# Attention of a fused attention and MLP kernel in 64-row and 64x64 TensorE tiles, with k and v loaded in two halves by two queues

## The chip, the cores and the metric

One core of a Trainium2 chip runs the whole kernel. The metric is the device time of one execution in microseconds (us). A run is called slow when it lies over 1.5% above the fastest run of the same kernel, and fast otherwise; fast runs are compared with fast runs taken in the same rounds of measurement.

## The reference

Eight batches of eight heads attend 576 queries to 72 pooled keys (means of eight neighbours), then an MLP with a tanh shrink follows. All tokens are independent in the MLP.

```python
B, H, S, D = q.shape                       # 8, 8, 576, 64
k_p = k.reshape(B, H, 72, 8, D).mean(axis=3)
v_p = v.reshape(B, H, 72, 8, D).mean(axis=3)
scores = np.matmul(q, k_p.transpose(0, 1, 3, 2)) / np.sqrt(D)
attn = softmax(scores)                     # cut: max, exp, sum
x = np.matmul(attn, v_p)                   # to (4608 tokens, 512)
h = x @ w_in                               # 512 -> 2048
out = (h - np.tanh(h)) @ w_out             # 2048 -> 512
```

## The kernel before

The MLP goes in nine groups of 512 tokens; one group is called a round here (round 0 is the start). A round has 64 wide matmuls for `h` and 64 for `o`. Between the `o` matmuls of round g the attention of batch g+1 is interleaved, for batches 2 to 7. GpSimd pools k and v; q, k and the attention result x are transposed by DMA.

```python
    def load_k(b):                                    # v: the same, with four small pieces
        return [
            load_main(k_pairs, k_raw[b % 2], b, 0, NM),   # 128 of the 144 rows of each pair of heads
            load_dense(k_pairs, k_raw[b % 2], b),         # the 16 rows left of each pair
        ]
    ...
    def score_mms(b, t, dst, c0, c1, pairs=range(NM)):
        for m in pairs if t == NM else (t,):
            ...                                       # KB: block-diagonal, two heads a tile
            nc.tensor.matmul(dst[p : p + w], lhsT=KB[b % 2][:, o : o + w],
                             rhs=qTs[b][:, m, c0:c1], start=True, stop=True)
    ...
    def av(b, blk, alloc, by_dma):                    # 2 x 3 matmuls of 130 columns a block
        x_sb = new_x()
        for half in range(2):
            av_half(b, blk, half, x_sb, alloc)        # matmuls, reciprocal, division
        if by_dma:
            ...
            nc.sync.dma_start_transpose(out=xT[:, :, pos : pos + 128 - p0], in_=...)
    ...
                if i == (3 if g == 1 else 8):         # in the h part of round g
                    k_dma_transpose(nb)
                    k_place(nb, nc.gpsimd.tensor_copy)
                    if nb + 1 < B:
                        load_k(nb + 1)
                        load_v(nb + 1)
                        load_q(nb + 1)
    ...
                    if 1 <= u <= NT:                  # in the o part, slot u of 16
                        scores(nb, u - 1)
                    if u in (7, 8, 9, 10, 12):
                        av(nb, (7, 8, 9, 10, 12).index(u), ps_b1, True)
```

The softmax here doesn't subtract the row's maximum and nothing guards it: scores larger than these inputs give would overflow.

## Time and profile before

| | before |
|---|---|
| median time | 300.64 us (300.51 to 300.65; a fourth run, beside the change, 301.79) |
| TensorE busy | 97% |
| next engine, VectorE | 53% |
| a round with attention | 30.81 us |
| of it the MLP | 27.63 us |

"Busy" of TensorE overlaps matmul with matmul, so distances between starts are the honest measure. The first lines are the DMA issues of the kernel before (name, issuing queue, count, size, median time to landing). Then come two stretches of four microseconds, with these columns: the stretch, its length, busy time and count of TensorE, its weight loads, VectorE, ScalarE and GpSimd, the granted clock, the DMA share and GB/s.

```profile
k_raw<-in_k_dram SPq DMA_DIRECT2D x7, 1024.0 KB, 5.9
q_raw<-in_q_dram SPq DMA_DIRECT2D x7, 1024.0 KB, 10.2
...
72.00:76.00 4.00, 4.00 (x28) 1.80 (x26) 0.00 (x0) 3.17 (x9) 0.00 (x0) 1.00 1.06 329
76.00:80.00 4.00, 4.00 (x34) 2.40 (x32) 2.31 (x9) 0.70 (x2) 1.15 (x1) 1.00 1.06 293
```

The loads of the next batch keep all DMA engines busy (share about 1) at some 300 GB/s while TensorE works on. They are hidden, but they are not idle time.

### The profile page before, as it was taken

To read this page: it belongs to the slowest core of one execution; us is meant where nothing else is said; L and a number is where in the kernel's file an instruction comes from. 1 tells how busy PE (TensorE), PEld (TensorE's weight loads), DVE (VectorE), ACT (ScalarE), POOL (GpSimd) and SP (SyncE) were. 2 spreads that over 40 slices of the span, in tenths; PEclk is the share of its full clock that TensorE was granted. 3 is DMA by queue.
4 is the path that set the end of the run, shared out by engine and by line. 5 is a ranking of instruction groups with operands and counts; after the bars stand their busy time and mean duration, and the time that the engine had idled before them with its cause. 6 is when DMAs were issued, how large, how long until landed. Compare 5 with 4: busy or idle time off the path is not lost.

```text
span 299.1 us, 4694 instructions
## 1 busy us (share of the span) xinstructions
PE 291.5 (97%) x1671; PEld 142.5 (48%) x1671; DVE 159.1 (53%) x343; ACT 149.4 (50%) x283; POOL 115.5 (39%) x110
## 2 busy tenths in 40 slices
PE   7989999999999999999999999999999999999994
PEld 3454455544544454445444554455445544444443
DVE  5658665673547444753476247716680758108600
ACT  4647583666146633654265516650665166126511
POOL 8500904871496109922971089307940000000000
PEclk9999999999999999999999999999999999999999
DMA  7999999849854998699648974897431430111032
GB/s 251 226 211 278 311 227 310 263 87 328 234 113 99 271 297 134 117 302 245 107 88 235 300 167 94 242 294 159 97 66 35 95 92 0 37 70 36 0 72 70
DMA packets 66183, 49.79 MB, mean 166 GB/s; under 512 B 39920, under 2 KB 52976, under 8 KB 66160
## 3 DMA queue, kind: packets, MB, share of 16 engines
q1 hardware_dynamic: 58832, 42.94, 56.0%
q0 software_dynamic: 4752, 4.72, 9.4%
q10 hardware_dynamic: 2576, 1.84, 2.3%
q8 instruction: 13, 0.21, 0.3%
q14 instruction: 10, 0.08, 0.1%
HBM read 36.70 MB, written 9.44 MB: 154 GB/s over the span
## 4 chain that ended last, share of the span: by engine, by line
PE 85%; DMA 9%; POOL 4%; issue 0%; SPq 0%; ACT 0%; DVE 0%; POOLq 0%
PE o_ps L456 40%; PE hT_ps L428 37%; DMA w1b<-in_moe_w_in_dram 4%; PE x_ps L346 4%; DMA k_raw<-in_k_dram 4%; PE s_ps L298 3%; POOL k_raw L198 1%; DMA out_dram<-o_sb 1%; POOL k_raw L203 1%; POOL kd L206 1%; POOL w2b L510 0%; PE xT_ps L390 0%; POOL v_raw L576 0%; PE qT_ps L171 0%; POOL w1b L503 0%
## 5 line engine op out<-in xcount | busy, mean ns | idle before, releaser
L456 PE MATMUL o_ps<-w2b,gT 128*128 128x512 bf16 x560 | 134.4, 380 | 0.0
L441 DVE TENSOR_TENSOR gT<-hT_ps,t_sb 128x512 bf16<-128x512 f32 x144 | 98.9, 691 | 57.7 <-ACT t_sb L439 57.6
L428 PE MATMUL hT_ps<-xT,w1b 128*128 128x512 bf16 x576 | 126.9, 379 | 0.3 <-ACT xT L397 0.3
L439 ACT ACTIVATE t_sb<-hT_ps 128x512 f32<-128x512 f32 x144 | 85.6, 597 | 38.3 <-PE hT_ps L428 37.5
L428 PEld LDWEIGHTS <-w1b 128*128 128x128 bf16 x576 | 55.9, 98 | 66.5 <-issue 0.4
L456 PEld LDWEIGHTS <-gT 128*128 128x128 bf16 x560 | 52.5, 98 | 52.0 <-issue 1.4
L465 ACT COPY o_sb<-o_ps 128x512 f32<-128x512 f32 x33 | 19.3, 585 | 75.2 <-PE o_ps L456 75.2
L359 DVE RECIPROCAL rden<-x_ps 128x4 f32<-128x4 f32 x80 | 14.2, 177 | 52.5 <-PE x_ps L346 52.0
L360 DVE TENSOR_TENSOR x_sb<-x_ps,rden 128x256 bf16<-128x256 f32 x80 | 34.0, 425 | 3.5 <-DMA xT<-x_sb 0.6
L148 POOL CAST q_bf<-q_raw 128x2048 bf16<-128x2048 f32 x6 | 11.3, 1888 | 59.9 <-issue 34.8
L198 POOL TENSOR_TENSOR k_raw<-k_raw 128x1280 f32<-128x1280 f32 x7 | 20.2, 2886 | 27.4 <-DMA k_raw<-in_k_dram 16.6
L317 ACT ACTIVATE E<-s_ps 128x288 bf16<-128x288 f32 x60 | 21.4, 410 | 13.2 <-PE s_ps L298 13.0
L346 PE MATMUL x_ps<-VB,E 128*128 128x130 bf16 x240 | 20.8, 221 | 0.4 <-ACT xT L397 0.3
L346 PEld LDWEIGHTS <-E 128*128 128x128 bf16 x240 | 16.9, 98 | 8.8 <-DVE VB L230 0.6
L216 POOL TENSOR_TENSOR v_raw<-v_raw 128x1280 f32<-128x1280 f32 x6 | 17.4, 2898 | 0.0
L298 PE MATMUL s_ps<-qT,KB 128*128 128x288 bf16 (+5 forms) x128 | 17.0, 290 | 0.2
L298 PEld LDWEIGHTS <-KB 128*128 128x128 bf16 (+1 forms) x128 | 7.0, 96 | 10.2 <-issue 3.5
L527 PE MATMUL warm_ps<-xT 128*128 128x512 bf16 x29 | 10.2, 465 | 1.3 <-DVE xT L539 1.3
L206 POOL TENSOR_TENSOR kd<-k_raw 128x640 bf16<-128x640 f32 x7 | 10.8, 1540 | 0.5
L203 POOL TENSOR_TENSOR k_raw<-k_raw 128x640 f32<-128x640 f32 x7 | 10.8, 1541 | 0.5
L397 ACT CAST xT<-xT_ps 128x256 bf16<-128x256 f32 (+1 forms) x14 | 5.8, 436 | 8.5 <-PE xT_ps L390 5.1
L219 POOL TENSOR_TENSOR v_raw<-v_raw 128x640 f32<-128x640 f32 x6 | 9.3, 1544 | 0.5
(73 smaller groups left out, 100.7 us busy)
## 6 DMA issues: line engine op xcount, KB each, us to landing
k_raw<-in_k_dram SPq DMA_DIRECT2D x7, 1024.0 KB, 5.9
q_raw<-in_q_dram SPq DMA_DIRECT2D x7, 1024.0 KB, 10.2
v_raw<-in_v_dram SPq DMA_DIRECT2D x7, 1024.0 KB, 9.3
out_dram<-o_sb SPq DMA_DIRECT2D x38, 128.0 KB, 2.4
out_dram<-o_sb SPq DMA_DIRECT2D x16, 256.0 KB, 3.7
w1b<-in_moe_w_in_dram POOLq DMA_DIRECT2D x4, 512.0 KB, 14.2
w2b<-in_moe_w_out_dram POOLq DMA_DIRECT2D x4, 512.0 KB, 16.9
k_raw<-in_k_dram SPq DMA_DIRECT2D x7, 128.0 KB, 5.8
```

What stands on the lines that cost most here:

```text
L198: first = eng.tensor_tensor(out=r[:, :, 0:4, :], in0=r[:, :, 0:4, :], in1=r[:, :, 4:8, :], op=ALU.add)
L216: eng.tensor_tensor(out=r[:, :, 0:4, :], in0=r[:, :, 0:4, :], in1=r[:, :, 4:8, :], op=ALU.add)
L298: nc.tensor.matmul(dst[p : p + w], lhsT=KB[b % 2][:, o : o + w], rhs=qTs[b][:, m, c0:c1], start=True, stop=True,)
L317: nc.scalar.activation(out=E[:, t, half * hs : (half + 1) * hs], in_=ps[:, :], func=ACT.Exp, scale=SCALE)
L346: nc.tensor.matmul(ps[:, 2 * n : 2 * n + 2, :].rearrange("p h d -> p (h d)") if n < 2 else ps.rearrange("p (a s) d -> p a s d", s=2)[:, :, ...
L359: nc.vector.reciprocal(out=rden[:, :, :], in_=ps[:, :, D:D1])
L360: nc.vector.tensor_tensor(out=x_sb[:, half, :, :], in0=ps[:, :, 0:D], in1=rden[:, :, :].to_broadcast([128, 4, D]), op=ALU.mult,)
L428: nc.tensor.matmul(h_tiles[i][:, :], lhsT=w1b[:, fb, i * 128 : (i + 1) * 128], rhs=xT[:, fb, tok0 : tok0 + TG], start=(fb == 0), stop=(fb ...
L439: nc.scalar.activation(out=t_sb[:, :], in_=h_ps[:, :], func=ACT.Tanh)
L441: nc.vector.tensor_sub(out=gT[:, :], in0=h_ps[:, :], in1=t_sb[:, :])
L456: nc.tensor.matmul(o_ps[:, :], lhsT=gts[i][:, tb * 128 : (tb + 1) * 128], rhs=w2b[:, i, :], start=(i == 0), stop=(i == NHID - 1),)
L465: (nc.vector.tensor_copy if g == 0 and tb % 2 else nc.scalar.copy)(out=o_sb[:, :], in_=o_ps[:, :])
```

## The change

The intent is to use the array better. A score tile of the kernel before has only two useful 64x64 blocks, so four heads go into four 64x64 tiles at once; AV contracts 64 rows, so two heads go into the two row halves at once. As each change of tile shape costs a drain, the work is gathered into four bursts a batch. For this each head must sit on one half of the partitions with 64 of its 72 rows. The source of such a tile has a hole of eight rows in the middle: as one pattern it would have four dimensions instead of three. The change issues k and v as two transfers of 64 partitions each, one by each of two queues. In batch 0, division runs over two PSUM banks at a time.

```diff
+    k_main = k_rows.rearrange("b (t i g) n -> b i g t n", i=2, g=G)[:, :, 0:GM]
+    v_main_rows = v_rows.rearrange("b (i t g) n -> b i g t n", i=2, g=G)[:, :, 0:GM]
...
+    def load_halves(src, left, dst, b):
+        for i, eng in enumerate((nc.sync, nc.gpsimd)):
+            yield eng.dma_start(out=dst[64 * i : 64 * i + 64, 0:NM, :], in_=src[b, i])
+        yield nc.sync.dma_start(out=dst[::2, NM, :], in_=left[b])
...
-        nc.sync.dma_start(
-            out=t[:, :, 0:R, :], in_=q[b, :, 0:QA, :].rearrange("h (p j) d -> p h j d", j=R)
-        )
+        n = H // 2 if b > 1 else H
+        for h in range(0, H, n):
+            nc.sync.dma_start(...)                     # q in two transfers of four heads
...
+    def score_main(b, j, dst, c0, c1):
+        for s, i in ((0, 0), (1, 1), (0, 1), (1, 0)):
+            m = j + 2 * i
+            nc.tensor.matmul(
+                dst[s][64 * i : 64 * i + 64],
+                lhsT=kTs[b][64 * s : 64 * s + 64, m, 64 * s : 64 * s + 64],
+                rhs=qTs[b][64 * s : 64 * s + 64, m, c0:c1],
...
+    def av_tiles(b, blk, pss):                         # 4 pairs of 65 columns, 1 pair of 260
+        ...
+                lhsT=E[64 * i : 64 * i + 64, t, c0 : c0 + 128],
...
-                    if 1 <= u <= NT:
-                        scores(nb, u - 1)
-                    if u in (7, 8, 9, 10, 12):
-                        av(nb, (7, 8, 9, 10, 12).index(u), ps_b1, True)
+                    if u in (2, 5):
+                        scores_pairs(nb, u // 3)
+                    if u in (7, 10):
+                        av_stream(nb, (0, 1, 2) if u == 7 else (3, 4))
```

Cut: the masks of the left-over rows, the pooling of v without duplicates, the fixed PSUM banks, and batch 0.

More of the change, by code (lines that the diff above doesn't have):

```diff
@@ L33 @@
 NM = 4
+GM = 64
+GL = 2 * (G - GM)
 SCALE = 1.0 / (POOL * float(D) ** 0.5)
@@ L57, with bank, __init__, tile @@
     opool = ctx.enter_context(tc.tile_pool(name="opool", bufs=4))
-    ps_h = ctx.enter_context(tc.tile_pool(name="ps_h", bufs=3, space=PSUM))
-    ps_o = ctx.enter_context(tc.tile_pool(name="ps_o", bufs=2, space=PSUM))
-    ps_a = ctx.enter_context(tc.tile_pool(name="ps_a", bufs=3, space=PSUM))
+    psum = ctx.enter_context(tc.tile_pool(name="psum", bufs=1, space=PSUM))
+    PS = psum.tile([128, 8, 512], FP32, name="PS")
+    def bank(i, shape):
+        n = 1
+        for d in shape[1:]:
+            n *= d
+        v = PS[:, i, 0:n]
+        if len(shape) == 3:
+            return v.rearrange("p (a b) -> p a b", a=shape[1])
+        if len(shape) == 4:
+            return v.rearrange("p (a b c) -> p a b c", a=shape[1], b=shape[2])
+        return v
+    class Banks:
+        def __init__(self, *ids):
+            self.ids, self.n = ids, 0
+        def tile(self, shape, dtype=None, name=None, tag=None):
+            self.n += 1
+            return bank(self.ids[(self.n - 1) % len(self.ids)], shape)
+    ps_h = Banks(0, 1, 4)
+    ps_o = Banks(2, 3)
+    ps_a = Banks(5, 6, 7)
     ctx.enter_context(tc.manual_schedule())
@@ L69 @@
     v_pairs = v_rows.rearrange("b (t r) n -> b r t n", r=PR)
+    k_main = k_rows.rearrange("b (t i g) n -> b i g t n", i=2, g=G)[:, :, 0:GM]
+    v_main_rows = v_rows.rearrange("b (i t g) n -> b i g t n", i=2, g=G)[:, :, 0:GM]
+    k_left = k_rows.rearrange("b (h g) n -> b h g n", g=G)[:, :, GM:G]
+    v_left_rows = v_rows.rearrange("b (h g) n -> b h g n", g=G)[:, :, GM:G]
     w1b = const.tile([128, NFB, DFF], BF16, name="w1b")
@@ L81 @@
     warm = const.tile([128, 1], FP32, name="warm")
+    mask4 = const.tile([128, NM, 1], FP32, name="mask4")
+    kmask = const.tile([128, 1, GL], FP32, name="kmask")
+    KL = [const.tile([128, NM, 32], BF16, name=f"KL{i}") for i in range(2)]
+    VS = [const.tile([128, NM, D1], BF16, name=f"VS{i}") for i in range(2)]
+    VL = [const.tile([128, NM, D1], BF16, name=f"VL{i}") for i in range(2)]
+    x0 = const.tile([128, 4, 2, 4, D], BF16, name="x0")
     VB = [const.tile([128, 3 * NM, D1], BF16, name=f"VB{i}") for i in range(2)]
@@ L113, in load_dense @@
         )
+    def load_halves(src, left, dst, b):
+        for i, eng in enumerate((nc.sync, nc.gpsimd)):
+            yield eng.dma_start(out=dst[64 * i : 64 * i + 64, 0:NM, :], in_=src[b, i])
+        yield nc.sync.dma_start(out=dst[::2, NM, :], in_=left[b])
     def load_k(b):
+        if b > 1:
+            return list(load_halves(k_main, k_left, k_raw[b % 2], b))
         return [
@@ L121, in load_v @@
     def load_v(b):
-        return [load_main(v_pairs, v_raw[b % 2], b, 0, NM)] + load_left(
-            v_pairs, v_raw[b % 2], b
-        )
+        return list(load_halves(v_main_rows, v_left_rows, v_raw[b % 2], b))
     def load_q_tail(b, t, eng):
@@ L134, in load_q @@
         t = q_raws[b]
-        nc.sync.dma_start(
-            out=t[:, :, 0:R, :], in_=q[b, :, 0:QA, :].rearrange("h (p j) d -> p h j d", j=R)
-        )
+        n = H // 2 if b > 1 else H
+        for h in range(0, H, n):
+            nc.sync.dma_start(
+                out=t[:, h : h + n, 0:R, :],
+                in_=q[b, h : h + n, 0:QA, :].rearrange("h (p j) d -> p h j d", j=R),
+            )
         if tail:
@@ L226, in pool_v, with pool_v_tiles @@
         v_left(VB[b % 2], r[:, NM, 0:1, :], eng)
+    def pool_v_tiles(b, eng):
+        r = v_raw[b % 2].rearrange("p t (j d) -> p t j d", d=D)
+        for n in (4, 2):
+            eng.tensor_tensor(
+                out=r[:, :, 0:n, :], in0=r[:, :, 0:n, :], in1=r[:, :, n : 2 * n, :], op=ALU.add
+            )
+        eng.tensor_tensor(
+            out=VS[b % 2][:, :, 0:D], in0=r[:, 0:NM, 0, :], in1=r[:, 0:NM, 1, :], op=ALU.add
+        )
+        eng.tensor_tensor(
+            out=r[:, NM, 0, :], in0=r[:, NM, 0, :], in1=r[:, NM, 1, :], op=ALU.add
+        )
+        eng.tensor_tensor(
+            out=VL[b % 2][:, :, 0:D],
+            in0=r[:, NM, 0:1, :].to_broadcast([128, NM, D]),
+            in1=mask4.to_broadcast([128, NM, D]),
+            op=ALU.mult,
+        )
     def v_main(vb, vs, eng, t0, t1):
@@ L279, in k_dma_transpose @@
     def k_dma_transpose(b):
-        kT = work.tile([128, NT, 128], BF16, name="kT", tag="kT", bufs=1)
+        kT = work.tile([128, NT, 128], BF16, name="kT", tag="kT")
         nc.sync.dma_start_transpose(
@@ L283, in k_dma_transpose @@
         )
+        nc.gpsimd.tensor_tensor(
+            out=KL[b % 2].rearrange("p t (c x) -> p t c x", x=2)[:, :, :, 0],
+            in0=kT[:, NM, :].rearrange("p (t c x) -> p t c x", t=NM, x=2)[:, :, :, 0],
+            in1=kmask.to_broadcast([128, NM, GL]),
+            op=ALU.mult,
+        )
         kTs[b] = kT
-    def k_place(b, eng):
-        kT = kTs.pop(b)
-        kb_main(KB[b % 2], kT[:, 0:NM, :], 0, NM, (eng, eng))
-        kb_left(KB[b % 2], kT[:, NM, :], eng)
     E_tiles = {}
@@ L304, in score_mms, with score_left, exp, new_E @@
             )
-    def scores(b, t):
-        if t == 0:
-            E_tiles[b] = work.tile([128, NT, S], BF16, name="E", tag="E")
-        E = E_tiles[b]
-        hs = S // 2
-        pss = []
-        for half in range(2):
-            ps = ps_a.tile([128, hs], FP32, name="s_ps", tag="ps_a")
-            score_mms(b, t, ps[:, :], half * hs, (half + 1) * hs)
-            pss.append(ps)
-        for half, ps in enumerate(pss):
-            nc.scalar.activation(
-                out=E[:, t, half * hs : (half + 1) * hs], in_=ps[:, :], func=ACT.Exp, scale=SCALE
-            )
+    def score_main(b, j, dst, c0, c1):
[5 more added lines that the diff above has]
+                rhs=qTs[b][64 * s : 64 * s + 64, m, c0:c1],
+                start=True,
+                stop=True,
+            )
+    def score_left(b, dst, c0, c1):
+        for m in range(NM):
+            nc.tensor.matmul(
+                dst[32 * m : 32 * m + 32],
+                lhsT=KL[b % 2][:, m, :],
+                rhs=qTs[b][:, m, c0:c1],
+                start=True,
+                stop=True,
+            )
+    def exp(out, in_):
+        nc.scalar.activation(out=out, in_=in_, func=ACT.Exp, scale=SCALE)
+    def new_E(b):
+        E_tiles[b] = work.tile([128, NT, S], BF16, name="E", tag="E")
+        return E_tiles[b]
+    def scores_pairs(b, j):
+        E = new_E(b) if j == 0 else E_tiles[b]
+        hs = S // 2
+        duos = [PS[:, b0 : b0 + 2, 0:hs] for b0 in (6, 0, 4)]
+        for h in range(2):
+            score_main(b, j, [d[:, h, :] for d in duos[0:2]], h * hs, (h + 1) * hs)
+        if j == 0:
+            for h in range(2):
+                score_left(b, duos[2][:, h, :], h * hs, (h + 1) * hs)
+        for t, d in zip((2 * j, 2 * j + 1, NM), duos if j == 0 else duos[0:2]):
+            exp(E[:, t, :].rearrange("p (h c) -> p h c", h=2), d)
     def scores_wide(b, ts):
@@ L336, in scores_tail, with av_mms @@
         )
-    def av_half(b, blk, half, x_sb, alloc):
+    def av_mms(b, blk, half, ps):
         E = E_tiles[b]
@@ L341, in av_half @@
         c0 = blk * 128 if blk < 4 else S - 128
-        ps = alloc([128, 4, D1], FP32, "x_ps")
         for n in range(3):
@@ L357, in av_half @@
             )
+    def av_half(b, blk, half, x_sb, alloc):
+        ps = alloc([128, 4, D1], FP32, "x_ps")
+        av_mms(b, blk, half, ps)
         rden = work.tile([128, 4, 1], FP32, name="rden", tag="rden", bufs=4)
@@ L365, in av_half, with av @@
         )
+    def av_tiles(b, blk, pss):
+        E = E_tiles[b]
+        vb, vl = VS[b % 2], VL[b % 2]
+        c0 = blk * 128 if blk < 4 else S - 128
+        mms = [
+            (pss[i][:, t, :], i, t, vb[64 * i : 64 * i + 64, t, :])
+            for t in range(NM)
+            for i in range(2)
+        ] + [
+            (
+                pss[i].rearrange("p t d -> p (t d)"),
+                i,
+                NM,
+                vl[64 * i : 64 * i + 64, :, :].rearrange("p t d -> p (t d)"),
+            )
+            for i in range(2)
+        ]
+        for n, (dst, i, t, rhs) in enumerate(mms):
+            nc.tensor.matmul(
+                dst,
+                lhsT=E[64 * i : 64 * i + 64, t, c0 : c0 + 128],
+                rhs=rhs,
+                start=(n < 2),
+                stop=(n >= len(mms) - 2),
+                skip_group_check=True,
+            )
     def new_x():
-        return work.tile([128, 2, 4, D], BF16, name="x_sb", tag="x_sb", bufs=4)
-    def av(b, blk, alloc, by_dma):
+        return work.tile([128, 2, 4, D], BF16, name="x_sb", tag="x_sb", bufs=6)
+    def av(b, blk, alloc):
         x_sb = new_x()
@@ L373, in av, with av_duo, av_norm, av_stream @@
             av_half(b, blk, half, x_sb, alloc)
-        if by_dma:
+        return x_sb
+    def av_duo(b, blk, b0, out):
+        ps = PS[:, b0 : b0 + 2, 0 : NM * D1].rearrange("p s (t d) -> p s t d", d=D1)
+        av_tiles(b, blk, [ps[:, i, :, :] for i in range(2)])
+        return ps, out
+    def av_norm(ps, out):
+        rden = work.tile([128, 2, NM, 1], FP32, name="rden2", tag="rden2")
+        nc.vector.reciprocal(out=rden[:, :, :, :], in_=ps[:, :, :, D:D1])
+        nc.vector.tensor_tensor(
+            out=out,
+            in0=ps[:, :, :, 0:D],
+            in1=rden[:, :, :, :].to_broadcast([128, 2, NM, D]),
+            op=ALU.mult,
+        )
+    def av_stream(b, blks):
+        xs = [new_x() for _ in blks]
+        duos = [
+            av_duo(b, blk, b0, x_sb[:, :, :, :]) for blk, b0, x_sb in zip(blks, (6, 0, 4), xs)
+        ]
+        for duo in duos:
+            av_norm(*duo)
+        for blk, x_sb in zip(blks, xs):
             p0 = 0 if blk < 4 else 64
@@ L380, in av @@
             )
-        return x_sb
     def x_pe_transpose(b, blk, x_sb, fbs=(0, 4)):
@@ L424, in mlp_h_mms @@
         if f0 == 0:
-            p, tag = pool or (ps_h, "hT_ps")
-            h_tiles[i] = p.tile([128, TG], FP32, name="hT_ps", tag=tag)
+            h_tiles[i] = ps_h.tile([128, TG]) if pool is None else pool
         for fb in range(f0, f1):
@@ L521, in after, with warm_pe @@
             )
-    warm_ps = ps_o.tile([128, 512], FP32, name="warm_ps", tag="o_ps")
-    def warm_pe(n, cols=512):
+    def warm_pe(n, cols=512, b0=3):
         for _ in range(n):
             nc.tensor.matmul(
-                warm_ps[:, 0:cols], lhsT=zeros[:, 0:128], rhs=zeros[:, 0:cols], start=True, stop=True
+                bank(b0, [128, cols]), lhsT=zeros[:, 0:128], rhs=zeros[:, 0:cols], start=True, stop=True
             )
@@ L589 @@
     nc.gpsimd.memset(KB[1][:, :], 0.0)
+    nc.gpsimd.memset(kmask[:, :, :], 0.0)
+    nc.gpsimd.memset(kmask[0:D, :, 0 : GL // 2], 1.0)
+    nc.gpsimd.memset(kmask[D:128, :, GL // 2 : GL], 1.0)
+    for i in range(2):
+        nc.gpsimd.memset(KL[i][:, :, :], 0.0)
+        nc.gpsimd.memset(VS[i][:, :, D:D1], float(POOL))
     q_raws[1] = raw.tile([128, H, R + 1, D], FP32, name="q_raw", tag="q_raw")
@@ L613, in q_turn, with v_pe_pool @@
         )
-    def v_pe_pool(t0, t1, turn):
-        ps = ps_any([128, t1 - t0, 1, D], FP32, "v_ps")
+    def v_pe_pool(t0, t1, turn, b0=None):
+        shape = [128, t1 - t0, 1, D]
+        ps = ps_any(shape, FP32, "v_ps") if b0 is None else bank(b0, shape)
         for j in range(POOL):
@@ L628, in ps_b1 @@
         return ps_a.tile(shape, dtype, name=name, tag="ps_a")
-    ps_all = ps_any
     q_turn(nc.scalar.copy, 0, 2)
@@ L655 @@
     v_left(VB[0], v_ps[:, 0, :, :], nc.vector)
-    vs = v_pe_pool(0, NM, ident)
+    vs = v_pe_pool(0, NM, ident, 4)
     v_main(VB[0], vs, nc.vector, 0, 2)
@@ L660 @@
     load_q_tail(1, q_raws[1], nc.scalar)
-    xs = [new_x() for _ in range(4)]
     gts = []
-    ps_o2 = lambda sh, dt, name: ps_o.tile(sh, dt, name=name, tag="o_ps")
-    ps_h2 = lambda sh, dt, name: ps_h.tile(sh, dt, name=name, tag="hT_ps")
-    warm_pe(2)
-    av_half(0, 0, 0, xs[0], ps_all)
-    av_half(0, 1, 0, xs[1], ps_all)
-    av_half(0, 2, 0, xs[2], ps_all)
-    x_pe_transpose(0, 0, xs[0], (0, 2))
-    av_half(0, 3, 0, xs[3], ps_all)
-    warm_pe(1)
-    x_pe_transpose(0, 1, xs[1], (0, 2))
@@ L673 @@
-    ps_any = ps_b1
-    av_half(0, 0, 1, xs[0], ps_h2)
-    warm_pe(1)
-    x_pe_transpose(0, 2, xs[2], (0, 2))
-    av_half(0, 1, 1, xs[1], ps_b1)
-    warm_pe(1)
-    x_pe_transpose(0, 3, xs[3], (0, 2))
-    av_half(0, 2, 1, xs[2], ps_o2)
-    mlp_h_mms(0, 0, 0, 2)
-    x_pe_transpose(0, 0, xs[0], (2, 4))
-    av_half(0, 3, 1, xs[3], ps_b1)
-    mlp_h_mms(0, 1, 0, 2)
-    x_pe_transpose(0, 1, xs[1], (2, 4))
-    mlp_h_mms(0, 2, 0, 2)
-    x_pe_transpose(0, 2, xs[2], (2, 4))
-    x_pe_transpose(0, 3, xs[3], (2, 4))
@@ L689, with av_pair @@
-    mlp_h_mms(0, 3, 0, 2, (ps_o, "o_ps"))
-    mlp_h_mms(0, 4, 0, 2, (ps_o, "o_ps"))
+    def av_pair(p, half, b0):
+        ps = PS[:, b0 : b0 + 2, 0 : 4 * D1].rearrange("p k (h d) -> p k h d", d=D1)
+        for k in range(2):
+            av_mms(0, 2 * p + k, half, ps[:, k, :, :])
+        rden = work.tile([128, 2, 4, 1], FP32, name="rden2", tag="rden2")
+        nc.vector.reciprocal(out=rden[:, :, :, :], in_=ps[:, :, :, D:D1])
+        nc.vector.tensor_tensor(
+            out=x0[:, 2 * p : 2 * p + 2, half, :, :],
+            in0=ps[:, :, :, 0:D],
+            in1=rden[:, :, :, :].to_broadcast([128, 2, 4, D]),
+            op=ALU.mult,
+        )
@@ new lines, in x0_turn @@
+    def x0_turn(blks, half, b0, eng):
+        n = len(blks)
+        ps = bank(b0, [128, 2, n, 128])
+        for i, blk in enumerate(blks):
+            for f in range(2):
+                nc.tensor.matmul(
+                    ps[:, f, i, :],
+                    lhsT=x0[:, blk, half, 2 * f : 2 * f + 2, :].rearrange("p h d -> p (h d)"),
+                    rhs=ident[:, :],
+                    start=True,
+                    stop=True,
+                )
+        c = blks[0] * 128
+        eng(
+            out=xT[:, 2 * half : 2 * half + 2, c : c + n * 128],
+            in_=ps.rearrange("p f i c -> p f (i c)"),
+        )
@@ new lines, in h_open @@
+    def h_open(i, b0):
+        mlp_h_mms(0, i, 0, 2, bank(b0, [128, TG]))
+    warm_pe(2, b0=3)
+    av_pair(0, 0, 2)
+    av_pair(1, 0, 5)
+    av_pair(0, 1, 0)
+    warm_pe(1, b0=4)
+    x0_turn((0, 1), 0, 7, nc.scalar.copy)
+    av_pair(1, 1, 2)
+    warm_pe(1, b0=4)
+    x0_turn((2, 3), 0, 5, nc.scalar.copy)
+    warm_pe(2, b0=4)
+    h_open(2, 4)
+    x0_turn((0, 1), 1, 7, nc.scalar.copy)
+    h_open(0, 0)
+    h_open(1, 1)
+    x0_turn((2,), 1, 5, nc.scalar.copy)
+    x0_turn((3,), 1, 6, nc.vector.tensor_copy)
@@ L691 @@
+    h_open(3, 2)
+    h_open(4, 3)
+    ps_any = ps_b1
+    ps_h.n = ps_o.n = 0
     nc.scalar.copy(out=q_bf[:QT, R, :, :], in_=t0[:QT, :, R, :])
@@ L703 @@
         if i == 11:
-            x4 = av(0, 4, ps_any, False)
+            x4 = av(0, 4, ps_any)
         if i == 13:
@@ L707 @@
     pool_k(1, nc.gpsimd, mid=(2, 3))
-    after(load_k(2), w2_dmas[2])
+    after(load_k(2)[::2], w2_dmas[2])
     load_v(2)
     load_q(2)
+    nc.vector.tensor_reduce(
+        out=mask4.rearrange("p (t c) o -> p t (c o)", t=2),
+        in_=ident.rearrange("p (i t c x z) -> p t c i x z", i=2, t=2, c=2, z=2)[
+            :, :, :, :, :, 0
+        ],
+        op=ALU.add,
+        axis=mybir.AxisListType.XY,
+    )
     o_pools = [(ps_o, "o_ps"), (ps_o, "o_ps"), (ps_h, "hT_ps"), (ps_h, "hT_ps")]
@@ L736 @@
             if u <= 13:
-                pend.append((u - 9, av(1, u - 9, ps_any, False)))
+                pend.append((u - 9, av(1, u - 9, ps_any)))
+    for i in range(2):
+        nc.gpsimd.tensor_scalar_mul(VL[i][:, :, D:D1], mask4[:, :, :], float(POOL))
     pool_k(2, nc.gpsimd)
     q_cast(2)
-    pool_v(2, nc.gpsimd)
+    pool_v_tiles(2, nc.gpsimd)
     q_dma_transpose(2)
@@ L751 @@
                     pool_k(nb, nc.gpsimd)
-                    pool_v(nb, nc.gpsimd)
+                    pool_v_tiles(nb, nc.gpsimd)
                 if i == (3 if g == 1 else 8):
                     k_dma_transpose(nb)
-                    k_place(nb, nc.gpsimd.tensor_copy)
                     if nb + 1 < B:
```

## The prediction

> **What bounds the kernel now.** I read the page first: busy shares, then the chain that ended last, then the costliest groups.
>
> ```profile
> PE 291.5 (97%) x1671; PEld 142.5 (48%) x1671; DVE 159.1 (53%) x343; ACT 149.4 (50%) x283; POOL 115.5 (39%) x110
> PE 85%; DMA 9%; POOL 4%; issue 0%; SPq 0%; ACT 0%; DVE 0%; POOLq 0%
> ...
> L456 PE MATMUL o_ps<-w2b,gT 128*128 128x512 bf16 x560 | 134.4, 380 | 0.0
> L428 PE MATMUL hT_ps<-xT,w1b 128*128 128x512 bf16 x576 | 126.9, 379 | 0.3 <-ACT xT L397 0.3
> L346 PE MATMUL x_ps<-VB,E 128*128 128x130 bf16 x240 | 20.8, 221 | 0.4 <-ACT xT L397 0.3
> ```
>
> The reader is to see that TensorE has almost no gap, and that no other engine passes 53%. Only what shortens TensorE's own stream shortens the kernel. The durations (380 ns) overlap, so I use the distance between starts instead: 64 of the wide matmuls take 13.81 us in the chain, 216 ns each.
>
> Next, the chain of waits in order of time for one steady round, here round 3:
>
> ```profile
> 116.75 13.81 PE hT_ps L428 x64
> 130.57 1.73 PE o_ps L456 x8
> 132.29 0.24 PE s_ps L298 x2
> 132.54 0.86 PE o_ps L456 x4
> ...
> 136.73 0.36 PE s_ps L298 x8
> 137.09 1.83 PE o_ps L456 x8
> 138.92 0.35 PE x_ps L346 x6
> 139.27 0.86 PE o_ps L456 x4
> ...
> 147.56 0.65 PE hT_ps L428 x3
> ```
>
> The round lasts 147.56 - 116.75 = 30.81 us, and its 128 MLP matmuls take 27.63. Attention of the next batch therefore costs **3.18 us** of TensorE a round: four score tiles of 0.245, the left-over scores 0.46, five AV blocks of 0.345 (0.98 + 0.46 + 1.73). There are six such rounds (batches 2 to 7). The chain is TensorE alone in all of them.
>
> The left-over scores are the only matmuls that already use narrow tiles (128x32). The timeline of TensorE around one burst of them:
>
> ```profile
> 104.89 1.03 PE L456 MATMUL o_ps<-w2b,gT 128*128 128x512 bf16 x4
> 105.85 0.43 PE L298 MATMUL s_ps<-qT,KB 128*32 128x288 bf16 x8
> 106.21 0.82 PE L456 MATMUL o_ps<-w2b,gT 128*128 128x512 bf16 x3
> ```
>
> The eight are two groups of four. Read start by start in the trace, the four of a group begin 3 to 4 ns apart and the second group begins 133 ns after the first: four concurrent matmuls cost what one of 288 columns costs (122 ns) plus about 11. But the first of them starts 308 ns after its wide predecessor instead of 216, and the wide one after the burst starts 218 ns after the last narrow one instead of 122, with 11 ns more behind it. So **each change of tile shape costs about 0.1 us**, 0.2 a visit.
>
> Last, the start of the kernel, from the chain again:
>
> ```profile
> 19.21 10.84 DMA k_raw<-in_k_dram
> ...
> 36.23 1.55 POOL kd L206
> 37.82 0.45 PE kT_ps L259 x5
> ```
>
> Batch 1's keys are loaded, pooled by GpSimd, and wanted by TensorE at 37.82 us, where it waits 0.52 us for them. Up to there the chain is DMA and GpSimd, not TensorE.
>
> **What the skill says.** "TensorEngine Tiling (Array Packing)", Tiling Modes, says that changing the tiling mode, not just the tile, drains the engine; this trace agrees, with 92 to 107 ns a change. "TensorE: Matmul & The Clock Gate", Part 3, says that matmuls on different tiles of the array run concurrently, some 4 ns apart; the trace shows 3 to 5 ns for column tiles. No instruction here shows it for row tiles, which is the main uncertainty. The same page, Back-to-back issue gap, gives about N / 2.4 + 2.5 ns; here 56 to 58 ns for 130 columns and 28 to 30 ns for 64, weight loads included. "DMA: Bandwidth & Descriptors", Issuing engines are not separate DMA queues, says that all queues end on the same 16 engines, so issuing from two saves only issue time. In before nearly all loads are on one queue; no run yet shows the split.
>
> **The change, part by part.**
>
> *Main scores.* Before, a 128x128 stationary tile of which only the two diagonal 64x64 blocks count is used four times, two halves of 288 columns each: 8 matmuls, 0.98 us. After, 16 matmuls of 64x64x288 in four groups of four. At the measured 133 ns a group: 0.53 us. Saves 0.45.
>
> *Left-over scores.* Still two groups of four 128x32 matmuls, 0.27 us plus changes of shape (counted below). Before 0.46 with its two changes.
>
> *AV.* Before, 6 matmuls of 130 columns a block, 0.345. After, 10 with 64 rows of contraction: four pairs of 65 columns and one pair of 260, the two of a pair in the two row halves. If a pair runs concurrently it costs (65 / 2.4 + about 4) = 31 ns, and the wide pair 112: 0.236 us a block (estimates from the spacings above), 1.18 for five against 1.73. Saves 0.55. If weight loads make the two of a pair wait for each other, some 58 ns a pair and 112 to 140 for the wide one: 0.34 to 0.37, nothing saved.
>
> *Changes of shape.* Before two a round. After, four bursts between wide matmuls give eight, and the first burst goes from 64x64 to 128x32 inside it: nine, at 0.097 to 0.1 each, 0.9 us. That is why the work is gathered into four bursts; scattered over ten places it would be twenty.
>
> *Sum of a round:* 0.53 + 0.27 + 1.18 + 0.9 = 2.88 us against 3.18. **It saves 0.30 a round, 1.8 us in six.** The nearly 1.0 us of saved streaming is mostly spent again on seven more drains.
>
> *Other engines in the steady rounds.* Exponentials become 5 of 576 columns instead of 10 of 288 (410 ns now; about 650 each by the 288-, 320- and 512-column rows). Five divisions of 512 columns (about 0.69 as the 128x512 TENSOR_TENSOR row, and 0.18 for the reciprocal) replace ten of 0.425 + 0.177: 4.4 instead of 6.0 us. GpSimd loses the placing of k (1.03) and about 1.0 of pooling v, and gains two DMA issues of 0.76. All of it is beside TensorE. The tightest hand-over is second score burst to AV: two exponentials after it, done about 1.7 us after the burst begins, against 0.3 to 0.4 of scores plus 8 wide matmuls of 1.73: hidden by about 0.4 us.
>
> *Batch 0.* Division goes from eight steps of 0.55 us to four of about 0.85 us, and xT is copied two blocks at a time. TensorE's own work in the stretch from 14.6 to 23.4 us is 6.6 us without fillers, so 2.2 us are fillers and waits. Following the new order I get the first hidden matmul at about 17.8 instead of 18.49 and the end of the stretch about 0.85 us earlier. But the next thing that binds is the pooled keys of batch 1 at 37.82, whose load starts when a weight load lands and which this change does not touch. TensorE arrives there earlier and waits 1.3 us instead of 0.5. **Gain at the end: 0.**
>
> Total: 300.6 - 1.8 = **298.8 us**.
>
> **Rivals.**
>
> 1. *Row tiles do not overlap.* For: every 64-row matmul still loads 128 columns of weights, ten loads a block instead of six, and no row-tiled matmul is in this trace. Against: full loads already follow each other every 28 to 30 ns, and four narrow loads start 3 ns apart. A round would cost about 3.4 to 3.56: plus 0.2 to 0.4, so 302 to 303 us.
> 2. *Row tiling needs no full drain*, or the inner change from 64x64 to 128x32 is cheap. Nothing in the trace speaks for it but nothing excludes it. Five changes instead of nine: 0.7 saved a round, 296.4 us.
> 3. *A load becomes the bound.* Half of k and v now sits in GpSimd's queue behind its own work, and each transfer covers 64 partitions. In before the DMA engines are full until about 55 us, then at 0.75 and less, and k of the next batch is ready 1.3 to 3.4 us before TensorE wants it. For: round 1 has GpSimd's half behind the last piece of w2. Against: the first burst comes one slot (0.86 us) later than before, GpSimd's chain is about 1.7 us shorter, and the bytes are the same. If it happens, one or two rounds lose 1 to 2 us: 300 to 302.
> 4. *The start counts after all*: if the keys of batch 1 come earlier, up to 0.85 us more: 298.
>
> **Range and chances.** The central case has perhaps 55%. Rival 1 has some 17%, rival 2 15%, a mild form of rival 3 10%. 2% would be 6.0 us, 1.0 us a round: that needs changes of shape that cost next to nothing, since 0.53 + 0.27 + 1.18 alone is 1.98. Slower by 2% would need several stalls of GpSimd or DMA. Range 296.3 to 301.4; chances 0.03 faster, 0.94 within 2%, 0.03 slower.
>
> **What the profile after would show.** Rounds of about 30.5 us instead of 30.81 in the chain. Score groups of four 64x64 starts a few ns apart, 133 ns from group to group. AV pairs about 31 ns apart, not 58. About 0.1 us at each of nine changes. TensorE's wait for the pooled keys near 37.8 us grown to about 1.3 us at the same instant. No wait of TensorE for ACT or DVE at AV, none for kT or KL. I am wrong in the mechanism if the pairs are 55 ns or more apart, if drains are far from 0.1 us, if round 1 or 2 shows a TensorE gap behind POOL or DMA, or if the kT burst moves from 37.8.

## The result, and the profile after

The changed kernel takes **310.45 us** (median of four, 309.66 to 314.68; the longest was a slow run). The ratio to the kernel before is 1.031, with a 95% interval of 1.026 to 1.036. A ratio is the mean time of one kernel's fast runs over that of the other's fast runs of the same rounds, so it is not quite the ratio of the medians.

First the page of the changed kernel: TensorE's busy share, then the chain that ended last by engine.

```profile
PE 292.2 (95%) x1840; PEld 134.6 (44%) x1840; DVE 150.4 (49%) x277; ACT 144.8 (47%) x249; POOL 114.7 (37%) x119
...
PE 67%; DMA 21%; POOL 6%; SPq 2%; issue 1%; DVE 1%; ACT 0%; POOLq 0%
```

TensorE's part of the chain fell from 85% to 67%, and DMA's rose from 9% to 21%. The matmuls themselves did what was hoped for. This is the timeline of TensorE in one undisturbed round (start, length, matmul, count):

```profile
171.97 0.44 PE L372 MATMUL PS<-qT,kT 64*64 64x288 bf16 x8
172.34 0.43 PE L382 MATMUL PS<-qT,KL 128*32 128x288 bf16 x8
172.70 2.76 PE L596 MATMUL PS<-w2b,gT 128*128 128x512 bf16 x12
...
177.60 0.30 PE L476 MATMUL PS<-VS,E 64*128 64x65 bf16 x8
177.74 0.27 PE L476 MATMUL PS<-VL,E 64*128 64x260 bf16 x2
177.85 0.29 PE L476 MATMUL PS<-VS,E 64*128 64x65 bf16 x8
```

Start by start in the trace, four 64x64 matmuls begin 3 to 4 ns apart, and the first of the next four 146 ns after the first of these. The two of an AV pair begin 3 to 4 ns apart, and pairs of 65 columns begin 29 to 39 ns apart. A block takes 0.24 to 0.25 us. The first matmul of a burst starts 309 to 312 ns after its wide predecessor instead of 216.

Between the bursts something new stands. The chain at the end of round 1, in order of time, and below it the same place in the kernel before:

```profile
72.94 14.64 DMA q_raw<-in_q_dram
...
87.64 2.69 DMA xT<-x_sb
...
90.39 15.67 PE PS L568 x64
```

```profile
83.36 2.59 PE o_ps L456 x12
85.95 13.81 PE hT_ps L428 x64
```

TensorE cannot begin round 2 before x of batch 2 has been transposed. That transpose was issued at 87.64, when the second half of q for batch 3 landed at 87.58. In the kernel before, the main load of q landed at 78.6 and round 2 began at 85.8. The link between the two transfers is the order of issue: in both traces an issue of this queue can be seen to go out just after the issue eight places ahead of it has landed (in the kernel before, q's tail left at 71.49, after k's load had landed at 71.47). The q half is eight places ahead of the third x transpose. The record does not say what makes the queue do so. The 64 matmuls after the gap take 15.67 us instead of 13.81: the trace shows a mean granted clock of 0.65 from 92 to 96 us, after the wait (0.5 for 3.4 us, from 91.4). The waits of the whole run give the sum (who waited for whom: total us, times, longest):

```profile
PE PS L568 <- DMA xT<-x_sb: 7.8, 4, 4.3
```

And the loads in the same stretches as before:

```profile
72.00:76.00 4.00, 4.00 (x38) 1.58 (x35) 0.00 (x0) 2.43 (x5) 0.53 (x1) 1.00 1.03 234
76.00:80.00 4.00, 4.00 (x46) 1.95 (x45) 1.86 (x6) 1.56 (x3) 0.00 (x0) 1.00 1.07 257
80.00:84.00 4.00, 4.00 (x38) 1.83 (x36) 2.35 (x5) 0.58 (x1) 0.00 (x0) 1.00 1.05 205
84.00:88.00 4.00, 2.10 (x10) 0.78 (x8) 0.00 (x0) 0.58 (x1) 0.36 (x1) 1.00 1.31 306
```

The DMA engines are as busy as before (share about 1) but move 205 to 257 GB/s instead of about 300, and need longer. The last half landed at 84.3; after that the rate is 306 again.

The starts of rounds 1 to 7 give the account. Before, each round is 30.81 us. After, they are 35.00, 34.02, 31.07, 30.55, 32.41 and 30.55: 8.76 us more in all. The gaps ahead of the first `h` matmul are 4.45, 1.77, 0.34 and 1.86, that is 8.42; the slow clock adds 1.7 and a wait of TensorE for VectorE in round 3 another 0.2; the undisturbed rounds save 0.26 each, 1.56 in six. 8.42 + 1.9 - 1.56 = 8.76.

### The profile page after: what moved, and what is told of

Same layout as the page of the kernel before. It is cut to its first block, busy times and chain, and to the rows that moved or that the text cites. A ratio compares the mean times of both kernels' runs of the same rounds, so it can differ in the third digit from the quotient of the medians.

```text
span 308.0 us, 4945 instructions
## 1 busy us (share of the span) xinstructions
PE 292.2 (95%) x1840; PEld 134.6 (44%) x1840; DVE 150.4 (49%) x277; ACT 144.8 (47%) x249; POOL 114.7 (37%) x119
## 4 chain that ended last, share of the span: by engine, by line
PE 67%; DMA 21%; POOL 6%; SPq 2%; issue 1%; DVE 1%; ACT 0%; POOLq 0%
PE PS L568 32%; PE PS L596 30%; DMA xT<-x_sb 6%; DMA q_raw<-in_q_dram 5%; DMA w1b<-in_moe_w_in_dram 4%; DMA k_raw<-in_k_dram 4%; DMA out_dram<-o_sb 2%; PE PS L476 2%; POOL v_raw L274 1%; PE PS L372 1%; POOL k_raw L241 1%; PE PS L433 1%; SPq L519 1%; PE PS L382 1%; POOL k_raw L246 1%
## 5 line engine op out<-in xcount | busy, mean ns | idle before, releaser
L568 PE MATMUL PS<-xT,w1b 128*128 128x512 bf16 x576 | 128.6, 382 | 8.3 <-DMA xT<-x_sb 7.8
L581 DVE TENSOR_TENSOR gT<-PS,t_sb 128x512 bf16<-128x512 f32 x144 | 98.8, 691 | 75.6 <-ACT t_sb L579 74.8
L596 PE MATMUL PS<-w2b,gT 128*128 128x512 bf16 x560 | 128.6, 379 | 0.0
L579 ACT ACTIVATE t_sb<-PS 128x512 f32<-128x512 f32 x144 | 85.6, 597 | 48.9 <-PE PS L568 48.1
L605 ACT COPY o_sb<-PS 128x512 f32<-128x512 f32 x33 | 19.4, 589 | 69.3 <-PE PS L596 61.9
L391 ACT ACTIVATE E<-PS 128x576 bf16<-128x576 f32 x30 | 17.6, 650 | 21.5 <-PE PS L372 21.5
L274 POOL TENSOR_TENSOR v_raw<-v_raw 128x1280 f32<-128x1280 f32 (+1 forms) x12 | 26.7, 2221 | 0.5
L502 DVE TENSOR_TENSOR x_sb<-PS,rden 128x512 bf16<-128x512 f32 x30 | 20.7, 692 | 1.0
L665 PE MATMUL PS<-xT 128*128 128x512 bf16 x30 | 10.2, 454 | 1.3 <-DVE xT L677 1.3
L476 PE MATMUL PS<-VS,E 64*128 64x65 bf16 x240 | 7.9, 191 | 0.0
```

The costliest lines, as they stand in the source:

```text
L274: eng.tensor_tensor(out=r[:, :, 0:n, :], in0=r[:, :, 0:n, :], in1=r[:, :, n : 2 * n, :], op=ALU.add)
L391: nc.scalar.activation(out=out, in_=in_, func=ACT.Exp, scale=SCALE)
L476: nc.tensor.matmul(dst, lhsT=E[64 * i : 64 * i + 64, t, c0 : c0 + 128], rhs=rhs, start=(n < 2), stop=(n >= len(mms) - 2), skip_group_check ...
L502: nc.vector.tensor_tensor(out=out, in0=ps[:, :, :, 0:D], in1=rden[:, :, :, :].to_broadcast([128, 2, NM, D]), op=ALU.mult,)
L568: nc.tensor.matmul(h_tiles[i][:, :], lhsT=w1b[:, fb, i * 128 : (i + 1) * 128], rhs=xT[:, fb, tok0 : tok0 + TG], start=(fb == 0), stop=(fb ...
L579: nc.scalar.activation(out=t_sb[:, :], in_=h_ps[:, :], func=ACT.Tanh)
```

## The experiments

My theory after the result (T): transfers of 64 partitions move bytes more slowly, so q lands later, and the x transposes behind it in the queue come too late. Rivals: the bunched AV is itself too late for x (A); the second queue is the disturbance, not the half partitions. The second run below calls T "T1" and this last rival "T2".

### Each column tile as one transfer of 128 partitions

```diff
-        for i, eng in enumerate((nc.sync, nc.gpsimd)):
-            yield eng.dma_start(out=dst[64 * i : 64 * i + 64, 0:NM, :], in_=src[b, i])
+        for t in range(NM):                            # source: 2 x 64 rows, one tile
+            yield nc.sync.dma_start(out=dst[:, t, :], in_=src[b, t])
```

> The changed kernel, but k and v of batches 2 to 7 come as four transfers of 128 partitions each (256 KB), all on the one hardware queue; same bytes, same tile layout, all matmuls as changed. Theory T (the half transfers of 64 partitions on two queues move bytes at some 205 to 257 GB/s where the kernel before has 293 to 351, so q lands late and the x transposes queued behind it land late): loads back at about 300 GB/s or more, no TensorE gap at the starts of rounds, rounds of 30.5 to 30.7 us, 298 to 300 us in all. Rival A (the bunched AV puts the x transposes too late by itself, the loads are innocent): still 307 to 311.

Measured: 504.79 us, ratio 1.678. Neither theory had it. One stretch shows the reason, with the columns as before:

```profile
65.00:70.00 5.00, 5.00 (x25) 2.24 (x23) 3.96 (x7) 3.41 (x7) 3.24 (x2) 1.00 0.13 50
```

The DMA share is 0.13 and the rate 50 GB/s, a level that the trace holds for some 35 us a batch. 0.13 is two sixteenths. The outermost dimension of these transfers counts 2 (the two heads), so I infer that the work was dealt to the engines along that dimension; the trace packs no engine numbers, so this is inferred and not shown. The run says nothing about T or A: it replaced a slow transfer by a far slower one.

### Both halves on one queue

```diff
-        for i, eng in enumerate((nc.sync, nc.gpsimd)):
+        for i, eng in enumerate((nc.sync, nc.sync)):
```

> The changed kernel, but both 64-partition halves of k and v are issued on the one hardware queue, one after the other. If half the partitions are what makes a transfer slow (T1): as slow or slower than the changed kernel, GB/s during loads under 250, 309 to 315 us. If the second, software-made queue is what disturbs (T2): loads at 300 GB/s or more again and 298 to 301 us.

Measured: 320.21 us, ratio 1.059 (1.052 to 1.067); the profiled run was a slow one, so its span is not used. Taking the second queue away made it worse, as T1 says. From 55 to 240 us, the load packets of 2048 bytes on this queue have a median of 160 ns against 84 ns in the kernel before. One stretch, with all the loads on one queue:

```profile
80.00:84.00 4.00, 4.00 (x37) 1.86 (x36) 3.03 (x9) 0.28 (x1) 0.00 (x0) 1.00 1.08 206
```

### The kernel before, with only its loads split by partitions

```diff
-            load_main(k_pairs, k_raw[b % 2], b, 0, NM),
+            eng.dma_start(out=dst[64 * i : 64 * i + 64, 0:NM, :],
+                          in_=src[b, 64 * i : 64 * i + 64, 0:NM, :])
+            for i, eng in enumerate((nc.sync, nc.gpsimd))
```

> The kernel before, its matmuls untouched, but the main transfers of k and v of batches 2 to 7 split in two 64-partition halves on the two queues as in the change. Theory T: the loads alone bring the loss, q lands 13 to 15 us after issue instead of 10, TensorE gaps at the starts of rounds 2 and 3, 304 to 311 us. Rival A (bunched AV): 300.6 as before, within 1 us.

Measured: 314.78 us, ratio 1.046 (1.043 to 1.048). The loads alone bring the loss, and more than the change had: the waits for x are longer here, and TensorE also waits 1.9 us for GpSimd's placing of the keys in round 1. So rival A falls as the cause of the loss: here AV is not bunched. q lands after 14.6 us at the median, instead of 10.2. The stretches and the waits of TensorE:

```profile
72.00:76.00 4.00, 3.70 (x20) 2.10 (x22) 0.00 (x0) 2.72 (x8) 1.58 (x4) 1.00 1.07 220
76.00:80.00 4.00, 4.00 (x30) 1.85 (x29) 0.70 (x3) 1.91 (x5) 0.00 (x0) 1.00 1.06 219
...
PE hT_ps L437 <- DMA xT<-x_sb: 9.6, 5, 4.4
...
PE s_ps L307 <- POOL KB L259: 1.9, 1, 1.9
```

### The kernel before, with its loads split by columns over the same two queues

The edit is shown against the run just above.

```diff
-                out=dst[64 * i : 64 * i + 64, 0:NM, :],
-                in_=src[b, 64 * i : 64 * i + 64, 0:NM, :],
+                out=dst[:, 2 * i : 2 * i + 2, :],
+                in_=src[b, 0:128, 2 * i : 2 * i + 2, :],
```

> The kernel before, with the main transfers of k and v of batches 2 to 7 split over the same two queues, but by columns: each half has all 128 partitions and two of the four tiles. If the half partitions are what is slow: loads near 300 GB/s and 300 to 302 us. If the second queue is what is slow: as with the split by partitions, 310 to 315 us.

Measured: 301.17 us, ratio 1.0015 (1.0001 to 1.0029), rounds of 30.81 us. It has the same two queues, the same number of transfers and the same bytes as the run above; only the halves are cut the other way. The stretch shows the rate of the kernel before:

```profile
72.00:76.00 4.00, 4.00 (x29) 1.89 (x28) 0.00 (x0) 2.90 (x8) 0.00 (x0) 1.00 1.04 328
```

This pair of runs settles it. Each against the kernel before of its own rounds, the one loses 13.9 us and the other 0.5: **the half partitions cost 13.3 us here, the second queue about 0.5.**

The Trainium skill has this. "SBUF — State Buffer", Door 1: The DMA port swizzle, says that partitions 0 to 63 reach only 8 of the 16 ports, and gives 196 GB/s for 64 partitions against 328 for 128 at 1 MiB. 205 to 257 GB/s with halves under way, against 293 to 351 with whole transfers, point the same way; the traces show no ports, so that part is the page's account and not shown here. The same page, "Can I just issue two DMAs to hit both halves?", answers no: two such transfers measured only 6% over one. That fits: the two queues together moved 208 to 220 GB/s in the run with the loads split by partitions, and one queue 203 to 206 in the run with both halves on it.

### q later

```diff
                     if u in (7, 10):
                         av_stream(nb, (0, 1, 2) if u == 7 else (3, 4))
+                    if u == 10 and nb + 1 < B:
+                        load_q(nb + 1)                # removed from the h part
```

> The changed kernel, with the q loads of the next batch issued after the x transposes (at the second AV burst) instead of before them; k and v loads still in slow halves. If the x transposes are late because their issue stands in order behind q loads that have not landed (the queue's in-order waits): x lands in time, TensorE gaps at round starts shrink from about 8 us in all to under 3, 300 to 305 us, though GpSimd gets q later and may delay the scores. If the x transposes are slow because the DMA engines are full whatever the order: gaps stay, 308 or more.

Measured: 334.99 us, ratio 1.113. The wait of TensorE for x is no longer among its large ones, so the first half of the expectation came true. But GpSimd got q late, everything behind that in its order came late too, and TensorE now waits in the scores:

```profile
PE PS L382 <- POOL KL L346: 12.2, 5, 3.1
```

It is a miss as a test: it removed one wait (x now costs TensorE 1.6 us, once) and made a larger one.

### The slow halves kept, the small loads first and q last

```diff
-                        load_k(nb + 1)
-                        load_v(nb + 1)
-                        load_q(nb + 1)
+                        load_all(nb + 1)   # left-over rows, q tail, k halves, v halves, q whole
```

> The changed kernel with its slow half transfers kept, but from batch 3 on the small loads are issued first and q last and whole, so that the issue eight places ahead of each of the first three x transposes is a q tail, a k half or a v half, and no longer a q load. If the queue's wait for its own eighth-last issue is what holds x (W): TensorE's gaps at round starts fall from 8.3 us to under 5 and the time to 303 to 307 us. If the x data stands behind q's bytes in the queue in any case (F): within 1.5 us of the changed kernel, 309 to 312.

Measured: 308.49 us, ratio 1.026 (1.0245 to 1.0276). W and F are two theories of how q holds x back: W through the wait for the issue eight places ahead, F through q's bytes alone. The time lies between them: 1.5 to 2 us better than the changed kernel, with gaps at round starts of 7.4 us instead of 8.4. The first x transpose left its queue at 81.76 us instead of 84.03, but the third at 87.22 instead of 87.64, right behind a half of v, which now stands eight places ahead. So this change of order is worth some 2 us at most; what remains fits slow bytes, as the next run confirms.

### The loads mended: one transfer of 128 partitions

The rows of two neighbouring heads are contiguous. Rows 8 to 135 of such a pair are the last 64 rows of one head and the first 64 of the next, 128 rows in one piece. Keys may be taken in any order, if v is taken in the same one. To keep four heads in four tiles, q is loaded by even and odd heads.

```diff
-        for i, eng in enumerate((nc.sync, nc.gpsimd)):
-            yield eng.dma_start(out=dst[64 * i : 64 * i + 64, 0:NM, :], in_=src[b, i])
+        nc.sync.dma_start(out=dst[:, 0:NM, :], in_=src[b, 8:136, :, :])
...
-                in_=q[b, h : h + n, 0:QA, :].rearrange("h (p j) d -> p h j d", j=R),
+                in_=q[b, i::2, 0:QA, :].rearrange("h (p j) d -> p h j d", j=R),
...
-                lhsT=kTs[b][64 * s : 64 * s + 64, m, 64 * s : 64 * s + 64],
+                lhsT=kTs[b][64 * s : 64 * s + 64, 2 * j + s, 64 * i : 64 * i + 64],
```

> The changed kernel with its loads mended: the main rows of k and v of batches 2 to 7 are 128 rows in one piece (rows 8 to 135 of each pair of heads: 64 of each head), so one transfer of 128 partitions and 1 MB each on the hardware queue, as in the kernel before; q is loaded by even and odd heads so that the four-tile scores keep their form. Matmuls and bursts as in the change. Theory T (half-partition transfers are the whole loss, TensorE's saving is as predicted): loads at 290 to 350 GB/s, no x gap at round starts, rounds of 30.5 us, 298.3 to 299.5 us, ratio 0.993 to 0.997 to the kernel before. If something else in the change also costs (fewer slots between q's issue and the x transposes): gaps at round 2 stay, 301 to 306.

Measured: 300.28 us (299.71 to 301.58), ratio 0.9986 (0.9967 to 1.0004), correct. The loss is gone with the half transfers, all matmuls and bursts as in the change. The rate in the stretches, then two round starts in the chain:

```profile
72.00:76.00 4.00, 4.00 (x38) 1.50 (x36) 0.00 (x0) 2.21 (x4) 0.00 (x0) 1.00 1.01 318
76.00:80.00 4.00, 4.00 (x49) 1.96 (x45) 1.53 (x4) 1.78 (x3) 0.00 (x0) 1.00 1.08 335
...
179.60 13.81 PE PS L588 x64
210.15 13.81 PE PS L588 x64
```

210.15 - 179.60 = 30.55 us a round, close to the predicted 30.5. Yet the median is 1.5 us above the prediction's 298.8. The profiled run, the slowest of the six, has rounds of 31.50, 30.91 and 30.73 us first, with gaps of 0.95 and 0.36 us, and begins round 1 0.8 us later than the kernel before.

### The same with batch 0 as before

The edit puts back the division and transposition of batch 0, one block at a time.

> The run above with batch 0 as in the kernel before (division one block at a time). Theory: batch 0's gain is swallowed by the wait for batch 1's pooled keys near 38 us, so the same time within 0.3 us. Rival: it is worth up to 0.85 us, then this is slower by that.

Measured: 300.81 us, ratio 1.0006 (0.9984 to 1.0028). The intervals of the two runs overlap, so a difference of 0.3 us is not resolved. In the profiles the old batch 0 begins round 1 at 54.84 us and the new one at 55.75: nothing speaks for a gain. Other profiles with the new batch 0 begin round 1 at 54.80 to 55.50, so the difference of these two is scatter as well.

### AV in five bursts instead of two

```diff
-                    if u in (7, 10):
-                        av_stream(nb, (0, 1, 2) if u == 7 else (3, 4))
+                    if u in (7, 8, 9, 10, 12):
+                        av_stream(nb, ((7, 8, 9, 10, 12).index(u),))
```

> The mended kernel with the five AV blocks of a batch in five bursts instead of two. If a change of tile shape costs 0.1 us: three more visits, 0.6 us a round, 3.6 us in all, so 302 to 303 us. If row tiles need no drain: within 0.5 us of the mended kernel.

Measured: 303.72 us, ratio 1.0105 (1.0085 to 1.0124), so 3.4 us above the mended kernel. Its undisturbed rounds are 31.18 to 31.19 us against 30.55: 0.63 us for three more visits, 0.21 each, 0.105 a change of shape. The estimate of the drain holds for row tiles, too. In this profile the gaps ahead of round starts are at most 0.11 us, where the mended kernel had 0.95 and 0.36. So bunched AV (rival A) may still have a part in the small rest; one profile of each does not show it.

### Three attempts to win the rest

The first issues the small loads first; the second puts the two large q loads on GpSimd's queue; the third puts k, v and q there.

```diff
-                nc.sync.dma_start(
+                (nc.gpsimd if b > 2 else nc.sync).dma_start(   # second: q; third: k and v too
```

> The mended kernel (whole transfers) with the small loads issued first and k, v, q after them. It has a rest of about 1.3 us in the starts of rounds 2 to 4. W: that rest goes, 298.6 to 299.4 us. F: unchanged, 299.9 to 300.6.

> The mended kernel with the two main q loads of batches 3 to 7 (all 128 partitions) on GpSimd's queue, k and v on the hardware queue. Neither W nor F can then hold x behind q: the rest of 1.3 us goes, 298.6 to 299.4 us, unless GpSimd's own chain, which now issues two more transfers, gets late (then over 300.5).

> The mended kernel with all large loads of batches 3 to 7 (k, v and q, every one over 128 partitions) on GpSimd's queue, so that the queue of the x transposes carries only the small pieces. If the scatter of the mended kernels (299.5 to 302.5 us) and the rest of about 1 us come from loads ahead of x in that queue: 298.6 to 299.5 us in all runs, rounds of 30.55 us throughout. If they come from GpSimd or the DMA engines themselves: 300 to 302.5 us again.

Measured: 302.36 us (ratio 1.0051), 300.38 us (1.0002, 0.9974 to 1.003) and 300.74 us (0.999, 0.997 to 1.0011). The first is worse, against both expectations. The second has a run of 299.47 us whose profile shows four rounds of 30.55 us and two of 30.84 and 30.73, but also runs up to 302.48. The third reaches 30.55 in most rounds, but has a gap of 1.42 us before round 3, again a wait for x. In it an x transpose took 4.51 us to land instead of about 2.5. So the rest of 1 to 1.5 us is **open**: the mended kernels scatter over some 1.4 to 3 us where the kernel before scatters over about 1, and I have not found what decides it. Where it falls is plain: the largest gap of each profile (0.95 us in the mended kernel, 1.52 with the old batch 0, 1.86 and 1.42 in the first and third run here) stands before round 2 or 3 and is a wait for an x transpose. None of them clearly beats the kernel before.

## Why the prediction was wrong

- **Main scores, AV, changes of shape: right.** Groups of four 146 ns apart (said: 133), so the four cost 0.58 us and not 0.53. Pairs 29 to 39 ns apart, 33 in the mean (31). A block 0.24 to 0.25 us (0.236). Changes of shape 0.08 to 0.11 us, confirmed by the run with five bursts at 0.105. An undisturbed round is 30.55 us (said: about 30.5), a saving of 0.26 instead of 0.30. Rivals 1 and 2 fell.
- **Batch 0: right within what the runs resolve.** The wait for batch 1's pooled keys grew to 1.3 us, as said, although the keys came at 38.21 instead of 37.82, and not "at the same instant".
- **The loads: this step failed.** The prediction said under rival 3: "the bytes are the same", and gave a mild form of it 10%. The bytes were the same, but the rate was not: 205 to 257 GB/s where there had been about 300. The prediction even wrote that "each transfer covers 64 partitions" and did not price it. It allowed one or two rounds a loss of 1 to 2 us; four rounds lost 8.42. One of its own signs of being wrong came true, a TensorE gap behind DMA at the end of round 1. It also read the DMA engines as at "0.75 and less" after 55 us. That is a mean over a whole round (and 0.86 in round 2); while the next batch loads, from 68 to 80 us, the share was already 1.02 to 1.06, so there was no room for slower loads. The size was there to be read in the skill's page on SBUF; I drew on its page on queues and stopped there.
- **Where the loss would show: wrong victim.** I compared the loads with the time at which GpSimd wants k, a slack of 1.3 to 3.4 us. What was hit first was not k but x: its transposes go by the same queue, behind the loads, and round 2 waits for them. I listed "no wait of TensorE for ACT or DVE at AV, none for kT or KL" and did not list xT. In the kernel before, q landed at 78.6 and round 2 began at 85.8, with x in between; that slack was in the trace and I did not work it out.
- **A consequence not foreseen:** after the 4.45 us wait the granted clock fell to 0.5 for 3.4 us, which cost about 1.7 us on top.
- **The size.** The run with only the loads split prices the loads alone at 13.9 us. The change lost 9.8. In the traces that run has 10.4 us of gaps at round starts and the 1.9 us wait for the keys, the change 8.4 and no such wait; why the change was hit less was not tested.

## What to carry to other kernels

A layout that suits TensorE is paid for by the transfer that makes it: before a tile is cut in half along the partitions, compare the load's rate at 64 and at 128 partitions, and look for a contiguous run of 128 rows that gives the same tile. A hidden load still has followers; ask what else stands in its queue and when the critical engine wants that, not only when the loaded data are wanted. When matmuls are made smaller, count the changes of tile shape first: here seven more changes of about 0.1 us gave back most of the one microsecond saved a round.

## What the Trainium skill lacked or had wrong

- "TensorEngine Tiling (Array Packing)", Tiling Modes, says that a change of mode drains the engine but gives no price. Here it is 0.08 to 0.11 us a change: 92 to 96 ns on entering a burst of 64x64, 64x128 or 128x32 tiles, 77 to 106 on leaving it or changing inside it.
- "DMA: Bandwidth & Descriptors", Issuing engines are not separate DMA queues, says that a second issuing engine saves only issue time. With whole transfers that holds: a second queue gained nothing (301.17 against 300.63 us). With half transfers, putting both on one queue cost more (320.21 us against 310.45); how much of that is order of issue was not separated. The section does not mention that a late load can hold back an unrelated transfer issued after it on the same queue: x waited for q, 4.45 us in one round.
